# Two weight splits of tick 21 are placed later, and six small products of expert 0 sooner, in a delta-rule and mixture-of-experts kernel

## The chip, the cores and the metric

The kernel runs on one core of a Trainium2 chip. The metric is the device time of one execution in microseconds (us); lower is better. The time before is 500.74 us, the median of 3 runs that lie between 495.13 and 504.34 us.

## The reference

The program computes a linear attention with the delta rule (4 sequences, 8 heads, 768 tokens, head size 48), then a mixture of 8 experts in which each of the 3072 tokens goes to one expert.

```python
k_n = k / (norm(k) + 1e-6)
for t in range(S):                                   # state: D x D for each sequence and head
    y[:, :, t] = q_t @ state
    v_old = state^T k_t
    state = state + beta_t * k_t (v_t - v_old)^T
x = y as (B*S, H*D) = (3072, 384)
e = argmax(x @ w_gate);  g = softmax(x @ w_gate)[e]
out = g * (relu(x @ w1[e]) @ w2[e])                  # w1: 384 x 1024, w2: 1024 x 384, 8 of each
```

## The kernel before

**The scan.** The 768 tokens are cut into 6 blocks of 128, a block of one sequence being a unit (24 units), and each unit into four parts of 32 tokens. A loop of 27 ticks (`for t in range(NN + LAG)`) runs skewed: in tick t, part q of unit t - q is worked on, so that four units are in flight. A tick on TensorE is: the products `ks` of `residual` (L438 with the state, L450 with the units' own updates); VectorE's subtraction of `ks` from the values `v_all` (L457); then `apply`, 64 small products of the solved triangle with `v_all` (L465), which ScalarE copies into the updates `u` (L469); then `finish` of unit t - 3, the output and state products (L488, L499, L508), ScalarE's copies `yt` (L512), and eight products that turn the output into token rows, `xp` (L532). Products `pq` for the next units (L279) are copied by ScalarE into `pm` (L289), which GpSimd masks (L290).

**The work beside it.** Every tick calls `beside(t, i)` for i = 0 to 6. Each call runs some steps of the routing of finished tokens (`emit_slots`: about a dozen VectorE operations that end in a slot number, `sli`, L590 to L615, and then one indirect DMA on GpSimd for each block of rows, which places the rows in the table `xg`, L540), then as many steps of `W` as the table `WSL` says, then steps of expert 0's early work as the table `ES` says. The order is written out by hand: each engine, and SyncE's queue of DMA issues, takes its instructions in program order.

**The weights.** `W` is the generator `pieces()`. A piece of a weight matrix is loaded as fp32 (L739), and `split` makes of it a rounded high part on ScalarE (L724) and the remainder on VectorE (L725), since each product is done as three products of parts. Three raw pieces are kept, so piece k + 3 is loaded behind piece k's split. Expert 0 has pieces 0 to 2 of `w1` (1024 columns) and 3 to 6 of `w2` (768 columns).

**Expert 0's beginning.** Its first 256 rows are worked on before the scan has ended. Their load from `xg` into `xr` (L761) is issued on SyncE behind the routing of unit 17 and waits until the rows placed so far have landed. `early()` transposes them in tick 23 (L816), does the hidden layer (L791, L794, L795) and the output layer (L802), which is made in two halves for the second 128 rows. `rest()` brings in the later rows: 128 by transposes (L854), and then a group of 64 by three products with the identity (L860) and three for each of the last two units, whose rows are taken from SBUF by a selection matrix `one` (L864). The string `EO` orders these steps: x, h and y are steps of `early`, t and o of `rest`; 13 of them stand in `ES`, the others run in the loop that drains the last routing, at the counts in `EF`.

**The experts.** Behind the scan, experts 0 to 7 run one after the other (`ffn`): the hidden layer in eight column groups into three PSUM tiles `hp`, each read by ScalarE and VectorE (`relu`, L794 and L795), and then the output layer (L802, L1146).

## Time and profile before

| what | value |
|---|---|
| median of 3 runs | 500.74 us (495.13 to 504.34) |
| the profiled execution's own time | 502.3 us |
| its span, first to last instruction | 500.5 us |
| mean granted TensorE clock | 0.959 |
| busy: PE, PEld, DVE, ACT, POOL | 92%, 85%, 65%, 53%, 33% |

The page cuts the span into 40 slices; TensorE is at nine tenths or more in nearly all slices of the second half (the experts), and at six to nine tenths in the first (the scan). PE is TensorE's products, PEld its weight loads, DVE is VectorE, ACT ScalarE, POOL GpSimd, SP SyncE, whose queue issues the direct DMAs. Between the span and the execution's own time lie 1.8 us.

### The profile page before, as it was taken

To read this page: it belongs to the slowest core of one execution; us is meant where nothing else is said; L and a number is where in the kernel's file an instruction comes from. 1 tells how busy PE (TensorE), PEld (TensorE's weight loads), DVE (VectorE), ACT (ScalarE), POOL (GpSimd) and SP (SyncE) were. 2 spreads that over 40 slices of the span, in tenths; PEclk is the share of its full clock that TensorE was granted. 3 is DMA by queue.
4 is the path that set the end of the run, shared out by engine and by line. 5 is a ranking of instruction groups with operands and counts; after the bars stand their busy time and mean duration, and the time that the engine had idled before them with its cause. 6 is when DMAs were issued, how large, how long until landed. Compare 5 with 4: busy or idle time off the path is not lost. (4 is left out here: it accounts for less than half of the span.)

```text
span 500.5 us, 17244 instructions
## 1 busy us (share of the span) xinstructions
PE 461.2 (92%) x7212; PEld 425.3 (85%) x7212; DVE 325.3 (65%) x728; ACT 265.6 (53%) x580; POOL 166.5 (33%) x342
## 2 busy tenths in 40 slices
PE   6969797989999799978899999999999999999995
PEld 4958686878887787867798999999999999999995
DVE  5999797698899989555644567465363638255330
ACT  4546694666666565767433356464454546354330
POOL 7002323767877878630211210111102020200202
PEclk9787897999999999999999799999999999999998
DMA  8798569467283433634302548464545637453101
GB/s 246 184 305 201 132 137 265 155 139 192 81 176 119 116 114 99 212 101 152 117 35 65 145 151 248 134 201 123 178 132 153 213 121 218 132 171 112 37 1 45
DMA packets 57147, 73.33 MB, mean 147 GB/s; under 512 B 25929, under 2 KB 44831, under 8 KB 57056
## 3 DMA queue, kind: packets, MB, share of 16 engines
q1 hardware_dynamic: 53600, 62.44, 44.5%
q0 software_dynamic: 3456, 9.57, 5.3%
q8 instruction: 71, 1.16, 0.9%
q14 instruction: 20, 0.16, 0.1%
HBM read 54.15 MB, written 18.62 MB: 145 GB/s over the span
## 5 line engine op out<-in xcount | busy, mean ns | idle before, releaser
L805 POOL DMA_INDIRECT out_dram<-yo,idx x32 | 30.7, 961 | 200.2 <-ACT yo L1140 101.0
L802 PE MATMUL y<-w2h,hx 128*128 128x384 f32 x352 | 93.6, 340 | 0.1
L725 DVE TENSOR_TENSOR w2l<-w2r,w2h 128x768 fp32r<-128x768 f32 x32 | 31.3, 980 | 73.8 <-ACT w2h L724 73.6
L802 PEld LDWEIGHTS y<-w2h,hx 128*128 128x128 f32 x352 | 64.0, 188 | 0.4 <-issue 0.4
L802 PE MATMUL y<-w2l,hx 128*128 128x384 f32 x176 | 59.2, 337 | 0.0
L791 PE MATMUL h<-xl,w1h 128*128 128x416 f32 (+2 forms) x168 | 57.3, 341 | 0.2 <-DVE xl L725 0.2
L791 PE MATMUL h<-xh,w1h 128*128 128x416 f32 (+2 forms) x168 | 57.3, 341 | 0.0
L791 PE MATMUL h<-xh,w1l 128*128 128x416 f32 (+2 forms) x168 | 57.2, 341 | 0.0
L469 ACT COPY u<-ks 32x384 f32<-32x384 f32 x96 | 45.1, 470 | 20.0 <-PE ks L465 18.5
L794 ACT ACTIVATE hx<-h 128x448 fp32r<-128x448 f32 (+1 forms) x64 | 32.9, 517 | 35.6 <-PE h L791 32.2
L1140 ACT ACTIVATE yo<-y,gt 128x384 f32<-128x384 f32 x22 | 12.8, 582 | 68.8 <-PE y L802 57.6
L795 DVE SCALAR_TENSOR_TENSOR hx<-h,hx 128x448 fp32r<-128x448 f32 (+1 forms) x64 | 37.1, 587 | 15.4 <-ACT hx L794 15.1
L290 POOL TENSOR_SCALAR_AFFINE_SELECT pm<-pm 128x1024 f32<-128x1024 f32 x24 | 27.5, 1148 | 56.6 <-ACT pm L289 56.3
L438 PE MATMUL ks<-st,kt 128*32 128x96 f32 x768 | 45.4, 256 | 0.6 <-issue 0.4
L279 PE MATMUL pg<-kt 64*128 64x128 f32 x384 | 34.8, 310 | 9.3 <-ACT gg L261 5.4
L279 PEld LDWEIGHTS pg<-kt 64*128 64x128 f32 x384 | 29.3, 208 | 12.3 <-ACT gg L261 6.3
L438 PEld LDWEIGHTS ks<-st,kt 128*32 128x32 f32 x768 | 33.7, 113 | 4.7 <-issue 1.5
L540 POOL DMA_INDIRECT xg<-row,sli x24 | 28.7, 1197 | 25.2 <-ACT yt L512 8.0
L261 ACT COPY gg<-pg 128x512 f32<-128x512 f32 x48 | 25.7, 587 | 21.4 <-PE pg L279 21.4
L465 PE MATMUL ks<-v_all,wt 32*32 32x48 f32 x1536 | 26.5, 204 | 10.4 <-DVE v_all L457 6.3
L725 DVE TENSOR_TENSOR w1l<-w1r,w1h 128x1024 fp32r<-128x1024 f32 x24 | 29.4, 1224 | 10.2 <-ACT w1h L724 10.1
L465 PEld LDWEIGHTS ks<-v_all,wt 32*32 32x32 f32 x1536 | 21.8, 105 | 15.0 <-DVE v_all L457 7.5
(196 smaller groups left out, 1057.8 us busy)
## 6 DMA issues: line engine op xcount, KB each, us to landing
w1r<-in_w_dram SPq DMA_DIRECT2D x24, 512.0 KB
w2r<-in_w_dram SPq DMA_DIRECT2D x32, 384.0 KB
xg<-zrow SPq DMA_DIRECT2D x7, 788.0 KB
kt<-in_kt_dram SPq DMA_DIRECT2D x17, 256.0 KB
xr<-xg SPq DMA_DIRECT2D x7, 591.0 KB
ku<-in_kn_dram SPq DMA_DIRECT2D x20, 192.0 KB
qt<-in_qt_dram SPq DMA_DIRECT2D x36, 96.0 KB
v_all<-in_v_dram SPq DMA_DIRECT2D x15, 192.0 KB
```

The costliest lines, as they stand in the source:

```text
L279: nc.tensor.matmul(pg[a][:, p], lhsT=kt[r, p], rhs=xt[r, p], start=True, stop=True, tile_position=(64 * a, 0), skip_group_check=True)
L290: nc.gpsimd.affine_select(out=pm, in_=pm, compare_op=ALU.is_gt, fill=0.0, base=0, pattern=[[0, H], [1, C]], channel_multiplier=-1)
L438: nc.tensor.matmul(ks[32 * q:32 * q + 32, 2 * p:2 * p + 2, :], lhsT=kt_t[n % KTL][:, p, 32 * q:32 * q + 32], rhs=st_view(n % B, p), start= ...
L465: nc.tensor.matmul(ks[r, h, :], lhsT=tiles[n // B]["wt"][r, n % B * H + h, :], rhs=vn[r, h, :], start=True, stop=True, tile_position=(32 * ...
L469: nc.scalar.copy(out=uview(n)[r], in_=ks[r])
L540: put = nc.gpsimd.indirect_dma_start(out=xg, out_offset=bass.IndirectOffsetOnAxis(ap=at, axis=0), in_=x, in_offset=None, bounds_check=OFF ...
L725: nc.vector.tensor_tensor(out=lo, in0=src, in1=hi.bitcast(F32), op=ALU.subtract)
L791: nc.tensor.matmul(ps, lhsT=w[:, d, fs], rhs=x_[:, d], start=(n == 0), stop=(n == len(terms) - 1))
L794: nc.scalar.activation(out=hh, in_=ps, func=AF.Relu)
L795: nc.vector.scalar_tensor_tensor(out=hl, in0=ps, scalar=0.0, in1=hh.bitcast(F32), op0=ALU.max, op1=ALU.subtract)
L802: nc.tensor.matmul(ps, lhsT=h(f)[h_], rhs=w2[w][:, f, :], start=(n == 0), stop=(n == len(terms) - 1))
L805: nc.gpsimd.indirect_dma_start(out=out, out_offset=bass.IndirectOffsetOnAxis(ap=idx, axis=0), in_=yo, in_offset=None, bounds_check=N - 1, ...
```

## The change

A piece's split becomes two steps of `W`: ScalarE's copy, then VectorE's subtraction with the next load. `WSL` gives both steps of most pieces the place they had together. Two places differ. Piece 1's split goes from (21, 3) to (21, 5), behind more of the routing's steps. Piece 2's copy stays at (21, 6), and its subtraction and load go to (22, 1), behind tick 22's `residual`. In `rest()`, the step with the small products is cut in two: `p` makes the products with the identity and those of the first of the two units, `o` those of the second unit and the split; `p` stands between the two halves of the last output layer of `early`. The experts' `run(W, 2)` takes both steps of a piece at the place where `run(W)` took one.

```diff
-    WSL = ((20, 3), (21, 3), (21, 6), (22, 3), (22, 6), (23, 3), (23, 6))
+    WSL = ((20, 3), (20, 3), (21, 5), (21, 5), (21, 6), (22, 1), (22, 3), (22, 3), (22, 6), (22, 6), (23, 3), (23, 3),
+           (23, 6), (23, 6))
-    EF = (4, 8, 9, 10, 12, 13, 14, 15)
-    EO = 'xxxhhhhhhhhytyyo'
+    EF = (4, 7, 8, 9, 10, 12, 13, 14, 15)
+    EO = 'xxxhhhhhhhhytypyo'
...
-            split(hi[:, j:j + st], lo[:, j:j + st], raws[k])
+            nc.scalar.copy(out=hi[:, j:j + st], in_=raws[k])
+            yield
+            nc.vector.tensor_tensor(out=lo[:, j:j + st], in0=raws[k], in1=hi[:, j:j + st].bitcast(F32), op=ALU.subtract)
             if k + AH < len(todo):
                 load(k + AH)
             yield
...
-        for i, (row, one) in enumerate(last):
+        for i in range(DEF):
+            if i == DEF - 1:
+                yield
+            row, one = last[i]
             for d in range(KD):
                 nc.tensor.matmul(pt[:, d], lhsT=row[:, d * 128:(d + 1) * 128], rhs=one, start=False,
-                                 stop=(i == len(last) - 1), skip_group_check=True)
+                                 stop=(i == DEF - 1), skip_group_check=True)
...
     def ahead_step():
-        if order and not (order[0] == "o" and len(last) < DEF):
-            run(other if order.pop(0) in "to" else ahead)
+        if order and len(last) >= {"p": 1, "o": DEF}.get(order[0], 0):
+            run(other if order.pop(0) in "tpo" else ahead)
...
-                run(W)
+                run(W, 2)
```

VectorE, ticks 21 and 22, before: `w1l` is the remainder of a piece of expert 0's first matrix (`w1r0_1` is piece 1, `w1r0_2` piece 2), `pos`, `ovr` and `sli` are the routing of units 16 and 17, and `ks22` is what tick 22 subtracts.

```order
L725 TENSOR_TENSOR w1l0_4189<-w1r0_1_4044,w1h0_4188 128x1024
L590 TENSOR_TENSOR pos4_0_4346<-base_77,pp4_0_4341 128x16
L592 TENSOR_TENSOR base_77<-base_77,pp4_0_4341 128x8
L598 TENSOR_TENSOR base_77<-base_77,jump_80 128x8
L600 TENSOR_TENSOR ovr4_0_4347<-pos4_0_4346,lim_78 128x16
L602 TENSOR_TENSOR ovr4_0_4347<-ovr4_0_4347,beyond_79 128x16
L603 TENSOR_TENSOR pos4_0_4346<-ovr4_0_4347,pos4_0_4346 128x16
L605 TENSOR_TENSOR pos4_0_4346<-pos4_0_4346,oh_all_84 128x16
L607 TENSOR_REDUCE sl_all_83<-pos4_0_4346 128x2
L615 CAST sli4_0_4380<-sl_all_83 128x2
L725 TENSOR_TENSOR w1l0_4189<-w1r0_2_4046,w1h0_4188 128x1024
L457 TENSOR_TENSOR v_all_109<-v_all_109,ks22_4386 128x384
```

The same place on VectorE in the changed kernel, from the last routing operation but one on.

```order
L608 TENSOR_REDUCE sl_all_83<-pos4_0_4342 128x2
L751 TENSOR_TENSOR w1l0_4189<-w1r0_1_4044,w1h0_4188 128x1024
L616 CAST sli4_0_4380<-sl_all_83 128x2
L458 TENSOR_TENSOR v_all_109<-v_all_109,ks22_4383 128x384
L535 TENSOR_REDUCE rl4_2_4429<-xp4_2_4430 128x8
L422 TENSOR_TENSOR v_all_109<-v_all_109,nt_all_120 128x384
L751 TENSOR_TENSOR w1l0_4189<-w1r0_2_4046,w1h0_4188 128x1024
L751 TENSOR_TENSOR w2l0_4505<-w2r0_0_4192,w2h0_4504 128x768
```

Piece 1's subtraction has moved from ahead of the routing operations to behind all of them but `sli`, and piece 2's from ahead of tick 22's subtraction to behind it and two more operations. On ScalarE the copy of piece 1 goes from ahead of tick 21's two `yt` copies to behind them, ahead of the `pm` copies; piece 2's copy stays.

SyncE's queue at the same ticks, before: `w2r0_0`, `w2r0_2`, `w2r0_4` and `w2r0_6` are pieces 3, 4, 5 and 6, `xr0` the first rows of expert 0.

```order
L739 DMA w2r0_0_4192<-in_w2_dram 128x2x384
L195 DMA qt5_115<-in_qt_dram 48x512 x2
L739 DMA w2r0_2_4339<-in_w2_dram 128x2x384
L739 DMA w2r0_4_4384<-in_w2_dram 128x2x384
L761 DMA xr0_4446<-xg_60 128x2x394
L739 DMA w2r0_6_4508<-in_w2_dram 128x2x384
```

SyncE's queue in the changed kernel.

```order
L740 DMA w2r0_0_4192<-in_w2_dram 128x2x384
L196 DMA qt5_115<-in_qt_dram 48x512 x2
L740 DMA w2r0_2_4365<-in_w2_dram 128x2x384
L764 DMA xr0_4443<-xg_60 128x2x394
L740 DMA w2r0_4_4446<-in_w2_dram 128x2x384
L740 DMA w2r0_6_4508<-in_w2_dram 128x2x384
```

Piece 5's load now stands behind the load of the rows, which waits for placed rows.

TensorE at the end of expert 0's early work, before: `y0_1` is the output of the second 128 rows (here the end of its second half), `xt4` the small products, `h0` the hidden layer of expert 0's other rows.

```order
L802 MATMUL y0_1_5186<-w2h0_4504,he7_5028 128x384
L802 MATMUL y0_1_5186<-w2l0_4505,he7_5028 128x384
L802 MATMUL y0_1_5186<-w2h0_4504,he7_5028 128x384
L860 MATMUL xt4_5232<-ident_67,xr0_4446 128x64 x3
L864 MATMUL xt4_5232<-one2_5142,row5_2_5055 128x64 x3
L864 MATMUL xt4_5232<-one3_5228,row5_3_5168 128x64 x3
L791 MATMUL h0_5265<-xb0_5149,w1h0_4188 128x192
```

TensorE in the changed kernel, where the second half of `y0_1` begins.

```order
L588 MATMUL pp5_3_5199<-oh_all_84,ones_74 128x8
L863 MATMUL xt4_5205<-ident_67,xr0_4443 128x64 x3
L870 MATMUL xt4_5205<-one2_5142,row5_2_5055 128x64 x3
L805 MATMUL y0_1_5186<-w2h0_4504,he4_4929 128x384
L805 MATMUL y0_1_5186<-w2l0_4505,he4_4929 128x384
```

And where that half ends.

```order
L805 MATMUL y0_1_5186<-w2h0_4504,he7_5028 128x384
L805 MATMUL y0_1_5186<-w2l0_4505,he7_5028 128x384
L805 MATMUL y0_1_5186<-w2h0_4504,he7_5028 128x384
L870 MATMUL xt4_5205<-one3_5235,row5_3_5168 128x64 x3
L794 MATMUL h0_5265<-xb0_5149,w1h0_4188 128x192
```

Two thirds of the small products have moved ahead of the second half; the last third and the hidden layer stay behind it.

## Rows read from the trace of the kernel before

**Rows 1.** The page, busy time and share of the span by engine.

```profile
PE 461.2 (92%) x7212; PEld 425.3 (85%) x7212; DVE 325.3 (65%) x728; ACT 265.6 (53%) x580; POOL 166.5 (33%) x342
```

**Rows 2.** Windows: ticks 20, 21, 22, each from its L465; busy us, clock, DMA.

```profile
205.17:213.13 7.96, 7.45 (x217) 6.36 (x216) 2.44 (x4) 5.56 (x12) 5.95 (x14) 1.00 0.81 277
213.13:222.95 9.82, 7.22 (x222) 6.15 (x221) 6.48 (x21) 7.07 (x15) 2.47 (x2) 1.00 0.29 97
222.95:232.41 9.46, 8.21 (x217) 7.04 (x217) 3.20 (x6) 6.26 (x14) 2.83 (x4) 0.82 0.56 173
```

**Rows 3.** Timeline of PE, ticks 21 to 23: start, length, operation, wait.

```profile
217.72 0.86 PE L438 MATMUL ks<-st,kt 128*32 128x96 f32 x24
...
219.37 1.14 PE L532 MATMUL xp<-esel,yt 128*128 128x104 f32 x8
222.95 0.88 PE L465 MATMUL ks<-v_all,wt 32*32 32x48 f32 x64 [2.44 <-DVE v_all L457]
...
228.74 0.86 PE L438 MATMUL ks<-st,kt 128*32 128x96 f32 x24
...
232.41 0.88 PE L465 MATMUL ks<-v_all,wt 32*32 32x48 f32 x64 [0.88 <-DVE v_all L457]
...
233.82 0.44 PE L816 MATMUL xt<-ident,xr 128*128 128x128 f32 x2
```

**Rows 4.** Timeline of DVE, ticks 21 and 22.

```profile
217.66 1.23 DVE L725 TENSOR_TENSOR w1l<-w1r,w1h 128x1024 fp32r<-128x1024 f32 x1 [2.28 <-ACT w1h L724]
218.80 0.16 DVE L590 TENSOR_TENSOR pos<-base,pp 128x16 f32<-128x16 f32 x1
...
219.48 0.99 DVE L602 TENSOR_TENSOR ovr<-ovr,beyond 128x16 f32<-128x16 f32 x1
...
221.13 0.17 DVE L615 CAST sli<-sl_all 128x2 int32<-128x2 f32 x1
221.21 1.23 DVE L725 TENSOR_TENSOR w1l<-w1r,w1h 128x1024 fp32r<-128x1024 f32 x1
222.35 0.55 DVE L457 TENSOR_TENSOR v_all<-v_all,ks 128x384 f32<-128x384 f32 x1
```

**Rows 5.** Timeline of ACT, ticks 21 and 23.

```profile
216.58 1.04 ACT L724 CAST w1h<-w1r 128x1024 fp32r<-128x1024 f32 x1
217.65 0.65 ACT L512 COPY yt<-yp 128x256 f32<-128x256 f32 x2
218.19 1.09 ACT L289 COPY pm<-pq 128x512 f32<-128x512 f32 x2
...
235.47 0.83 ACT L724 CAST w2h<-w2r 128x768 fp32r<-128x768 f32 x1
```

**Rows 6.** Timeline of POOL, ticks 21 and 22.

```profile
219.35 1.09 POOL L290 TENSOR_SCALAR_AFFINE_SELECT pm<-pm 128x1024 f32<-128x1024 f32 x1 [6.29 <-ACT pm L289]
221.57 1.72 POOL L540 DMA_INDIRECT xg<-row,sli  x1 [1.13 <-DVE sli L615]
...
223.89 0.97 POOL L540 DMA_INDIRECT xg<-row,sli  x1 [0.16 <-issue]
```

**Rows 7.** Timeline of SP, its queue, at the load of expert 0's rows.

```profile
228.41 0.37 SPq L761 DMA_DIRECT2D xr<-xg  x1
```

**Rows 8.** Windows: the stretch behind that load; columns as in rows 2.

```profile
229.50:232.00 2.50, 2.03 (x70) 1.72 (x61) 1.32 (x2) 1.58 (x4) 1.09 (x1) 1.00 0.94 311
```

**Rows 9.** Timeline of PE behind the last small products.

```profile
276.45 1.55 PE L864 MATMUL xt<-one,row 128*128 128x64 f32 x12
278.41 0.92 PE L791 MATMUL h<-xb,w1h 128*128 128x192 f32 x2 [0.41 <-ACT xb L724]
```

**Rows 10.** Windows: expert 0's hidden layer of the later rows, in two stretches.

```profile
278.41:285.50 7.09, 7.05 (x32) 6.88 (x33) 5.61 (x25) 2.40 (x5) 1.27 (x7) 0.52 0.55 154
285.50:290.00 4.50, 4.50 (x42) 4.50 (x41) 3.68 (x13) 2.87 (x8) 0.00 (x0) 1.00 0.73 223
```

**Rows 11.** Timeline of DVE, first read of a hidden tile in that layer.

```profile
282.62 0.36 DVE L795 SCALAR_TENSOR_TENSOR hx<-h,hx 128x192 fp32r<-128x192 f32 x1
```

## The prediction

> **What bounds the kernel now.** I read the page's busy shares first: TensorE is busy 92% of the span [rows 1], and no other engine comes near it, so the kernel ends when TensorE has got through its list, and only what TensorE waits for, or what slows its clock, can be won. I then cut the scan into ticks with the windows view, to see whether the ticks that the change touches are longer than their neighbour. They are: tick 20 takes 7.96 us, tick 21 9.82 and tick 22 9.46, with less TensorE work done per us [rows 2]. The timeline of TensorE names why. Between its last product of tick 21 (L532, from 219.37, 1.14 long) and L465 of tick 22 it stands for 2.44 us, and the trace puts that down to VectorE's subtraction L457 [rows 3]. Then the granted clock falls: it averages 0.82 over the next tick, after 1.00 in the two before [rows 2].
>
> VectorE's timeline shows what L457 stood behind. Piece 1's remainder ran at 217.66, having waited for ScalarE's copy; the routing's small operations came behind it from 218.80 to 221.13; then piece 2's remainder from 221.21; and L457 only at 222.35 [rows 4], though what it subtracts was complete before L532 began at 219.37. None of the work ahead of it is needed by TensorE in tick 22. The second place is expert 0's later rows: behind the small products (twelve of the eighteen instructions take 1.55 us) TensorE waits 0.41 for a copy [rows 9], and then the clock stands at 0.52 for 7.09 us before it is back at 1.00 [rows 10].
>
> **Part one: the wait of tick 22.** In the new order the routing operations start as soon as their products are there, about 2 us before 218.80, and end before piece 1's copy does. ScalarE does the two `yt` copies first (0.65) and then piece 1's copy (1.04) [rows 5]; if `yt` starts where the copy started, at 216.6, or a tenth later when its products are done, the copy ends between 218.3 and 218.5. Piece 1's remainder takes 1.14 to the next operation's start (217.66 to 218.80) [rows 4], so `sli` starts near 219.6 and L457, next behind it, near 219.7; it takes 0.55 and is done at 220.3. TensorE's L532 ends at 220.5. So the wait goes whole: **-2.4 us**. What hides piece 1's remainder now is TensorE's own list from L438 at 217.72 to L532; without that cover it would cost up to its 1.23. Piece 2's remainder, 1.23 us, goes behind L457 and two more operations, into a stretch where VectorE is busy for 3.20 of 9.46 us [rows 2]; nobody needs it before the hidden layer, which comes behind the transposes of tick 23. It costs nothing. ScalarE's `pm` copies come 0.3 later, and GpSimd's mask with them: that is work for a later tick.
>
> **The clock of tick 22.** From L465 to the next L438 tick 21 took 4.59 us (213.13 to 217.72) and tick 22 5.79 (222.95 to 228.74) [rows 2, 3]: 1.2 more, a lower bound since tick 21 has small routing products there that tick 22 lacks. The upper bound is the clock's own: 0.82 over 9.46 us is 3.4 us at half rate, half of it, 1.7, lost [rows 2]. The fall came behind the only wait over 2 us here, and the wait of 0.88 at 232.41 [rows 3] has full-rate work behind it. I take **-1.5 us**.
>
> **What is late next.** Everything behind tick 22 then comes 3.9 us sooner, if its data do. The wait of 0.88 at tick 23's L465 [rows 3] stays, since piece 4's split keeps its place. The new candidate is the load of expert 0's rows, which TensorE transposes at 233.82 [rows 3], so at 229.9 in the changed kernel. The load was issued at 228.41 [rows 7], 4.5 us behind the second placing DMA at 223.89 [rows 6], and had landed by 232.0 together with a weight piece of similar size [rows 8]; the two share 2.5 us, so the rows alone landed between 231.0 and 232.0, 2.6 to 3.6 behind the issue. In the new order `sli` is there 1.3 us sooner, but GpSimd masks until 220.8 (219.35 + 1.09 [rows 6], plus the 0.3), so the first placing DMA starts at 220.8 in place of 221.57 and the second at 222.4 to 223.1 in place of 223.89, the first having taken 0.97 to 1.72 [rows 6]. The rows' load is then issued at 226.9 to 227.6 and landed at 229.5 to 231.2: a new wait between nothing and 1.3 us. The early end is nearer, because piece 5's load, which ran while the placed rows were being written, is now queued behind. I take **+0.3 us**.
>
> SyncE's queue is the other thing to look at: piece 5's load used to be issued before the rows' load, and now it waits with it. It would be issued near 227.5 and land third at most 3.6 to 4.5 later, 231.1 to 232; ScalarE wants it at 235.47 [rows 5] less 3.9, at 231.6. That is cover of half a us or a lack of as much, on an engine that is not the bound. Piece 6, behind it, has a whole half tick more.
>
> **Part two: the small products.** Twelve instructions move ahead of the output layer's second half and six stay. TensorE's work is the same, so nothing is won directly, and the 0.41 wait for the copy stays [rows 9]. What can be won is the clock: 7.09 us at 0.52 are 3.4 us lost [rows 10]. The fall follows the longest run of 64-column products in the neighbourhood and a wait; the change cuts that run in three. I think it more likely than not that the clock then holds. But the 3.4 us are not all to be had. The hidden layer fills three PSUM tiles, and VectorE reads the first only at 282.62 to 282.98 [rows 11], 4.6 us behind the layer's start at 278.41, because a list of small operations that count the experts' rows stands ahead. At full rate (42 instructions in 4.50 us [rows 10], so 0.96 for the nine of a tile) three tiles are full after 2.9 us, and TensorE stands for 1.7. That leaves 1.7 of the 3.4. The last block's rows are also placed later, behind the output's DMA on GpSimd, by up to the length of what was moved (1.6 us: twelve instructions, at the rate of [rows 9]), and expert 1's load waits for them; if that shows, it takes more of this. Bounds: 0 and -3.4; I take **-1.0 us**.
>
> The experts' `run(W, 2)` leaves the order of every engine as it was: nothing.
>
> **A rule against the change.** VectorE's L602 ran 0.99 us where its like take 0.16 to 0.17, from 219.48 to 220.47, while GpSimd's mask ran from 219.35 to 220.44 [rows 4, 6]; it ended when the mask did. The Trainium skill says why, in "SBUF — State Buffer", section "Who interferes with whom": VectorE and GpSimd share a pair of SBUF ports as an exclusive lock, taken by an operation with two SBUF inputs or, in a faster mode, by a copy or cast, and the second to come stands until the first ends. This row agrees for two SBUF inputs; no run here shows a cast. By that rule `sli`, a cast, could meet the mask.
>
> As a mechanism of this kernel that is a rival. `sli` starts at 219.6 and the mask at 219.7. If the mask comes first, `sli` stands until 220.8, L457 runs to 221.4, and TensorE waits 0.95 us: the first term is -1.5 and not -2.4. L457 itself reads PSUM, and ran 0.55 in its normal place as here.
>
> **The sum.** -2.4 - 1.5 + 0.3 - 1.0 = -4.6 us. The profiled execution took 502.3 us; it would take 497.7. It lies 1.6 above the median of 500.74, so the median would be **496.1 us**.
>
> **The rivals.** *All of it.* Both falls of the clock go and nothing is given back: -2.4 - 1.7 - 3.4 = -7.5, 493.2 us. For it speaks that the runs before reach down to 495.13, so the falls may not be in every run; against it the three PSUM tiles.
>
> *A part.* `sli` meets the mask, and the clock of expert 0 falls as before: -1.5 - 1.5 + 0.3 = -2.7, 498.0 us. For it speaks L602; and the small products that stay, with the copy's wait behind them, are still 1.2 us of low work.
>
> *The wait only moves.* The rows land at the late end, TensorE waits 1.3 in tick 23, and tick 22 keeps 0.95: -1.5 - 1.2 + 1.3 = -1.4, 499.3 us.
>
> *Slower.* SyncE's queue decides. If the placed rows land no sooner than before, the rows' load is issued at 228.4 and TensorE stands from 229.9 until 231.0 to 232.0, at the worst 2.1 us; a wait of that length brought the clock down in tick 22, 1.5 more; and piece 5 lands third, a us behind the rows, at 233.0, which holds ScalarE's copies behind it for 1.4. Together 5.0 against the 3.9 won: +1.1, 501.8 us. It decides from a rows' issue later than 228. Against it: the placing DMAs can start sooner.
>
> **How the numbers follow.** The forecast has 0.45, all of it 0.18, a part 0.22, the wait only moved 0.09, slower 0.06. The runs before spread by 9 us, and a median of a few such runs moves by 2 or 3 by itself, which is wider than the unknown terms. With the cases from 493.2 to 501.8 the range is 491.5 to 500.8 us. A measurement of this kernel can tell some 2% (10 us) from no change; none of the cases is that far off, so within 2% gets 0.92, faster 0.06, for all of it in a good draw of the clock elsewhere, and slower 0.02.
>
> **What the changed profile would show.** Right: no wait at tick 22's L465, tick 21 near 7.4 us, the granted clock at 1.00 through tick 22, L465 of tick 23 near 228.5; the rows' load issued near 227 and a wait of less than 0.5 at the transposes; the hidden layer at full clock with a new wait on VectorE before its fourth tile. Wrong: `sli` as long as GpSimd's mask; a wait of over 1 us at L816; clock at half behind the small products as before.

## The result, and the profile after

The changed kernel took 502.16 us (median of 22 runs, 498.52 to 505.65) beside 500.4 us of the kernel before on the same chip. The ratio is 1.0057, with a 95% interval of 1.0033 to 1.008: a little slower, where 496.1 was predicted, and outside the predicted range. (The ratio compares fast runs alone, and the profiled execution of the kernel before, 502.3 us, counts among the slow ones; the medians of all runs are 1.8 us apart.) Run again on another chip it came out at 1.0046 [1.0006, 1.0085].

The page says little: TensorE's share is what it was [rows 1].

```profile
PE 459.6 (92%) x7212; PEld 422.8 (84%) x7212; DVE 325.5 (65%) x728; ACT 264.8 (53%) x580; POOL 166.8 (33%) x342
```

The two executions have to be cut where the change begins. Up to tick 21's `xp` product (L532 before, L533 after) both kernels have the same instructions, and yet the eighteen profiles of this study reach that product between 204.8 and 213.7 us, with falls of the clock in different places. What lies in front of it says nothing of the change. So I count from the start of the `xp` product of tick 21, by which I mean the one directly ahead of tick 21's `apply` (212.06 us before, 212.65 changed); the prediction, which cuts at `apply`, has it at the end of tick 20. First the kernel before, by windows: ticks 21 and 22 together, tick 23, the three ticks up to the last `xp` product, and the rest to the end. Columns as in [rows 2], with GB/s last.

```profile
212.06:230.39 18.33, 15.35 (x437) 13.19 (x436) 8.51 (x23) 12.50 (x27) 5.61 (x7) 0.91 0.40 113
230.39:240.07 9.68, 7.88 (x204) 6.33 (x203) 6.76 (x22) 6.45 (x16) 1.49 (x2) 1.00 0.51 173
240.07:270.18 30.11, 28.25 (x399) 25.09 (x393) 14.52 (x61) 12.13 (x31) 5.68 (x6) 1.00 0.22 66
270.18:500.48 230.30, 223.71 (x1304) 220.13 (x1304) 116.20 (x223) 103.31 (x177) 32.54 (x39) 0.98 0.45 138
```

The same four stretches of the changed kernel.

```profile
212.65:229.22 16.57, 14.92 (x437) 12.39 (x436) 8.67 (x23) 11.57 (x26) 5.74 (x7) 1.00 0.41 126
229.22:239.61 10.39, 7.87 (x203) 6.33 (x202) 6.77 (x22) 7.15 (x17) 1.89 (x2) 1.00 0.54 176
239.61:269.75 30.14, 28.26 (x399) 25.09 (x394) 14.51 (x61) 12.12 (x31) 5.67 (x6) 1.00 0.21 66
269.75:501.34 231.59, 222.55 (x1304) 218.85 (x1304) 116.27 (x223) 103.11 (x177) 32.50 (x39) 0.99 0.44 137
```

The change wins 1.76 us in ticks 21 and 22, loses 0.71 in tick 23 and 1.29 behind the scan: +0.27 in all, less than the 1.8 us between the medians and the 2.9 of the ratio. In the last stretch TensorE is busy for 1.16 us less (the clock stands higher), but idle for 9.04 us in place of 6.59. The second profile of the changed kernel has the same first and last stretch, and in tick 23 a fall of the clock to its lower level, 1.2 GHz (0.66 on the tick's average), with which the tick takes 3.1 us more:

```profile
207.44:224.00 16.56, 14.59 (x438) 12.31 (x437) 8.68 (x23) 11.59 (x26) 5.75 (x7) 1.00 0.36 119
224.00:237.51 13.51, 11.56 (x204) 9.41 (x203) 8.20 (x23) 7.51 (x17) 3.43 (x3) 0.66 0.42 146
267.41:498.91 231.50, 222.37 (x1304) 218.68 (x1304) 116.19 (x223) 103.19 (x177) 32.70 (x39) 0.99 0.42 137
```

Where TensorE stood, by its timeline in the changed kernel (answers to [rows 3, 9]): 0.51 us in place of 2.44 in tick 22, then three short stops; 1.59 in place of 0.88 in tick 23; and a new wait of 2.12 us before the fourth hidden tile of expert 0, on VectorE's `hx`.

```profile
221.60 0.70 PE L466 MATMUL ks<-v_all,wt 32*32 32x48 f32 x44 [0.51 <-DVE v_all L458]
222.63 0.46 PE L466 MATMUL ks<-v_all,wt 32*32 32x48 f32 x20 [0.34 <-issue]
...
224.33 0.27 PE L489 MATMUL yp<-qt,st 64*64 64x128 f32 x1 [0.30 <-issue]
225.01 0.61 PE L500 MATMUL sum<-u,ku 128*64 128x48 f32 x15 [0.41 <-ACT u L470]
...
227.57 0.86 PE L439 MATMUL ks<-st,kt 128*32 128x96 f32 x24
...
231.96 0.88 PE L466 MATMUL ks<-v_all,wt 32*32 32x48 f32 x64 [1.59 <-DVE v_all L458]
...
277.87 0.75 PE L794 MATMUL h<-xb,w1h 128*128 128x192 f32 x2 [0.41 <-ACT xb L725]
...
283.52 0.47 PE L794 MATMUL h<-xb,w1h 128*128 128x192 f32 x2 [2.12 <-DVE hx L798]
...
291.02 0.42 PE L805 MATMUL y<-w2h,hx 128*128 128x384 f32 x1
```

VectorE's timeline names what stood ahead (answers to [rows 4, 11]): in tick 22 the cast `sli`, 1.06 us long where it took 0.17 before; in tick 23 piece 4's remainder; in expert 0 the list of small operations that count the experts' rows (`cnt` to `tot`).

```profile
218.89 1.23 DVE L751 TENSOR_TENSOR w1l<-w1r,w1h 128x1024 fp32r<-128x1024 f32 x1 [1.03 <-ACT w1h L749]
220.03 1.06 DVE L616 CAST sli<-sl_all 128x2 int32<-128x2 f32 x1
221.00 0.54 DVE L458 TENSOR_TENSOR v_all<-v_all,ks 128x384 f32<-128x384 f32 x1
...
230.22 1.22 DVE L751 TENSOR_TENSOR w2l<-w2r,w2h 128x768 fp32r<-128x768 f32 x1 [1.41 <-ACT w2h L749]
231.36 0.54 DVE L458 TENSOR_TENSOR v_all<-v_all,ks 128x384 f32<-128x384 f32 x1
...
280.21 0.17 DVE L1199 TENSOR_TENSOR cnt<-base,e 128x8 f32<-128x8 f32 x1 [0.71 <-issue]
280.56 0.34 DVE L1205 TENSOR_TENSOR cmpt<-cnt,thr 128x168 f32<-128x168 f32 x1 [0.18 <-POOL itr L1213]
...
283.11 0.36 DVE L798 SCALAR_TENSOR_TENSOR hx<-h,hx 128x192 fp32r<-128x192 f32 x1
```

GpSimd's timeline has the two causes (the first line answers to [rows 6]): the mask ran beside the cast, and the constants `e` and `thr`, which the counting needs, stood behind an output transfer that the later second half of the output layer had made late. It begins 0.13 us ahead of the hidden layer's first product; in the kernel before, at 276.61, it began 1.80 ahead [rows 9].

```profile
219.90 1.17 POOL L291 TENSOR_SCALAR_AFFINE_SELECT pm<-pm 128x1024 f32<-128x1024 f32 x1 [5.41 <-ACT pm L290]
...
277.74 0.98 POOL L808 DMA_INDIRECT out_dram<-yo,idx  x1 [6.18 <-ACT yo L847]
279.02 0.97 POOL L541 DMA_INDIRECT xg<-row,sli  x1 [0.31 <-DVE kind L1163]
280.00 0.17 POOL L1198 IOTA e<- 128x8 f32 x1
280.09 0.43 POOL L1203 IOTA thr<- 128x168 f32 x1
```

### The profile page after: what moved, and what is told of

The parts are those of the page before. It is cut to its first block, busy times and chain, and to the rows that moved or that the text cites. A ratio compares the mean times of both kernels' runs of the same rounds, so it can differ in the third digit from the quotient of the medians.

```text
span 501.3 us, 17245 instructions
## 1 busy us (share of the span) xinstructions
PE 459.6 (92%) x7212; PEld 422.8 (84%) x7212; DVE 325.5 (65%) x728; ACT 264.8 (53%) x580; POOL 166.8 (33%) x342
## 3 DMA queue, kind: packets, MB, share of 16 engines
q8 instruction: 71, 1.16, 1.0%
## 5 line engine op out<-in xcount | busy, mean ns | idle before, releaser
L280 PE MATMUL pg<-kt 64*128 64x128 f32 x384 | 36.0, 319 | 10.6 <-DMA kt<-in_kt_dram 5.0
L439 PE MATMUL ks<-st,kt 128*32 128x96 f32 x768 | 44.4, 253 | 0.2
L280 PEld LDWEIGHTS pg<-kt 64*128 64x128 f32 x384 | 30.4, 217 | 13.3 <-ACT gg L262 4.1
L439 PEld LDWEIGHTS ks<-st,kt 128*32 128x32 f32 x768 | 32.7, 111 | 4.0 <-issue 0.9
L466 PE MATMUL ks<-v_all,wt 32*32 32x48 f32 x1536 | 26.8, 206 | 8.9 <-DVE v_all L458 4.3
L466 PEld LDWEIGHTS ks<-v_all,wt 32*32 32x32 f32 x1536 | 22.2, 107 | 13.8 <-DVE v_all L458 6.1
```

The source lines that it names most:

```text
L280: nc.tensor.matmul(pg[a][:, p], lhsT=kt[r, p], rhs=xt[r, p], start=True, stop=True, tile_position=(64 * a, 0), skip_group_check=True)
L439: nc.tensor.matmul(ks[32 * q:32 * q + 32, 2 * p:2 * p + 2, :], lhsT=kt_t[n % KTL][:, p, 32 * q:32 * q + 32], rhs=st_view(n % B, p), start= ...
L466: nc.tensor.matmul(ks[r, h, :], lhsT=tiles[n // B]["wt"][r, n % B * H + h, :], rhs=vn[r, h, :], start=True, stop=True, tile_position=(32 * ...
```

## The experiments

They ran on four chips, numbered 1 to 4, with 12 runs of every kernel and 35 of the kernel before on each chip; ratios are to the kernel before on the same chip. "21+22" and "23" are ticks as cut above, "rest" goes from the last `xp` product to the end, "sum" from tick 21's product to the end; "wait" is TensorE's on `hx` in expert 0's later rows. These five come from the one profiled execution, in us. The changed kernel itself ran on chip 2 and on the chip of the first comparison only, so that e3, e9 and e16 are set against its ratio on other chips.

| kernel | chip | ratio [95%] | 21+22 | 23 | rest | sum | wait |
|---|---|---|---|---|---|---|---|
| before | - | 1 | 18.33 | 9.68 | 230.3 | 288.4 | 0 |
| changed | - | 1.0057 [1.0033, 1.008] | 16.57 | 10.39 | 231.6 | 288.7 | 2.12 |
| e5 changed again | 2 | 1.0046 [1.0006, 1.0085] | 16.56 | 13.51 | 231.5 | 291.5 | 2.10 |
| e1 split alone | 1 | 0.9911 [0.9874, 0.9948] | 15.79 | 10.39 | 228.9 | 284.9 | 0 |
| e6 split again | 2 | 0.9933 [0.9896, 0.9969] | 16.56 | 10.39 | 230.5 | 287.5 | 1.09 |
| e15 split a third time | 4 | 0.995 [0.9909, 0.9991] | 15.16 | 10.39 | 230.6 | 286.1 | 1.09 |
| e2 small products alone | 1 | 0.9996 [0.9958, 1.0035] | 18.82 | 10.81 | 229.9 | 289.4 | 2.11 |
| e3 constants early | 1 | 0.996 [0.9917, 1.0003] | 16.77 | 10.38 | 229.4 | 286.4 | 1.22 |
| e4 piece 1 behind `sli` | 1 | 0.9953 [0.9917, 0.9989] | 15.92 | 10.92 | 228.9 | 285.6 | 1.08 |
| e7 e3, counting late | 2 | 1.0044 [1.0011, 1.0077] | 16.49 | 10.40 | 233.8 | 290.8 | 0.82 + 2.38 |
| e8 split, counting late | 2 | 1.0044 [1.0007, 1.008] | 17.86 | 9.67 | 234.7 | 292.4 | 2.73 |
| e9 changed, counting cut up | 3 | 0.9977 [0.9945, 1.0009] | 16.65 | 10.39 | 228.6 | 285.8 | 0.82 |
| e16 the same again | 4 | 0.9942 [0.9909, 0.9976] | 17.03 | 10.39 | 228.6 | 285.9 | 0.82 |
| e10 split, counting cut up | 3 | 0.9974 [0.9936, 1.0011] | 16.53 | 13.51 | 230.2 | 290.2 | 0 |
| e11 changed, piece 4 moved | 3 | 1.0087 [1.0042, 1.0131] | 16.53 | 9.92 | 232.9 | 289.5 | 2.10 |
| e12 e10, piece 4 moved | 3 | 0.9962 [0.9926, 0.9999] | 18.11 | 12.96 | 227.7 | 288.1 | 0 |
| e13 e9, casts on GpSimd | 4 | 0.995 [0.9911, 0.9989] | 17.67 | 10.39 | 229.3 | 287.3 | 0.82 |
| e14 split, casts on GpSimd | 4 | 0.9937 [0.9904, 0.9971] | 17.28 | 10.38 | 229.1 | 286.6 | 0 |

The letters of the theories are given afresh in each expectation.

### Which half costs: e1 and e2

The split alone goes back to the old small products (in `rest()` too; `ahead_step()` keeps its new test, which without a `p` in `EO` is the old one); the small products alone go back to the old places of the pieces. Other lines are left out here.

```diff
 e1
-    EF = (4, 7, 8, 9, 10, 12, 13, 14, 15)
-    EO = 'xxxhhhhhhhhytypyo'
+    EF = (4, 8, 9, 10, 12, 13, 14, 15)
+    EO = 'xxxhhhhhhhhytyyo'
 e2
-    WSL = ((20, 3), (20, 3), (21, 5), (21, 5), (21, 6), (22, 1), (22, 3), (22, 3), (22, 6), (22, 6), (23, 3), (23, 3),
+    WSL = ((20, 3), (20, 3), (21, 3), (21, 3), (21, 6), (21, 6), (22, 3), (22, 3), (22, 6), (22, 6), (23, 3), (23, 3),
```

Expected of e1: 

> The changed kernel with its new places for the weight splits, but expert 0's small products in one step behind the output layer, as before. Theory A (the moved small products cost: they push the output's DMA, the last rows' DMA and the constants behind them on GpSimd, and VectorE's counting waits for those; the splits gain a little): 1 to 2 us faster than the kernel before, ratio 0.996 to 0.998, wait of tick 22's L465 near 0.5 us in place of 2.4, the hidden layer of expert 0 as before. Theory B (the splits cost, by the blocked cast and the later loads; the small products gain by the clock): 1 to 3 us slower, ratio 1.002 to 1.006.

Expected of e2: 

> The kernel before's places for the weight splits, and the small products cut in two as in the changed kernel. Theory A: 2 to 4 us slower than before, ratio 1.004 to 1.008, with a wait of about 2 us of TensorE on VectorE before the fourth hidden tile of expert 0. Theory B: 1 to 3 us faster, ratio 0.994 to 0.998.

Measured: 0.9911 and 0.9996. The split wins about 4 us by itself, more than theory A had it (0.996 to 0.998). The small products win nothing and lose nothing, which lies in neither theory's range; they bring the wait of 2.11 us on `hx`, the same as in the changed kernel (2.12), but in this profile the clock holds at the hidden layer, ahead of the wait and behind it. The two halves don't add up to the 1.0057 of the whole.

### Whether chips differ: e5 and e6

The changed kernel and the split alone, unchanged, on one chip.

Expected of e5: 

> The changed kernel once more, beside the split alone on one chip. If the two halves add up (the split alone measured 0.991, the small products alone 1.000), it comes out at 0.990 to 0.996 of the kernel before, and the first comparison's 1.006 belongs to that chip's runs, not to the change. If the two halves together cost something that neither has alone, it comes out at 1.003 to 1.008 again, and tick 22 shows once more the 2 us in which ScalarE waits for tick 22's key product (9.3 us between marks, where the split alone has 7.3). The wait before the fourth hidden tile on VectorE's hx comes under both, at 1.5 to 2.2 us.

Expected of e6: 

> The split alone once more (the new places of the weight pieces, expert 0's small products as before). Theory A (the small products are what costs): 0.988 to 0.994 again, no wait on hx in expert 0, and at least 1 us from the changed kernel on the same chip. Theory B (the two kernels are one, and chips differ): within 0.3% of the changed kernel here.

Measured: 1.0046 and 0.9933. The result stands, and the small products cost some 1.1% next to the split (0.6% between the medians of all runs), more than alone. Tick 22 was no peculiarity of the changed kernel: the split alone has the same 16.56 us here, and 15.79 in its first profile. How long each of the two ticks is goes with the chip and not with the kernel: in all eight profiles of the chips 1 and 4 tick 21 is 7.9 to 10.6 us long and tick 22 6.9 to 8.6; in the other ten tick 21 is 7.31 and tick 22 9.2 to 11.0. And against the expectation the split alone has a wait on `hx` here, 1.09 us. The sums of the two profiles differ by some 4 us (287.5 and 291.5): 1.0 in the rest, 3.1 from the clock that fell in tick 23, which only the one profile shows.

### The constants, and the order of piece 1: e3 and e4

e3 writes GpSimd's six constants at tick 25, ahead of the late output transfer (`counters()` holds the moved lines, which are left out here). e4 is the split alone with piece 1's remainder behind the cast `sli`; the edits that it shares with e1 are left out too, and the "first kernel" of its expectation is e1.

```diff
 e3
+        if t == NN + 1:
+            counters()
 e4
-    WSL = ((20, 3), (20, 3), (21, 5), (21, 5), (21, 6), (22, 1), (22, 3), (22, 3), (22, 6), (22, 6), (23, 3), (23, 3),
+    WSL = ((20, 3), (20, 3), (21, 5), (21, 6), (21, 6), (22, 1), (22, 3), (22, 3), (22, 6), (22, 6), (23, 3), (23, 3),
```

Expected of e3: 

> The changed kernel, with the six constants that GpSimd writes behind the last rows' DMA (e0, thr, itr, part, wo1, wo2) written in tick 25 instead. Theory A: VectorE's counting no longer waits for GpSimd, expert 0's first hidden tile is read about 0.9 us sooner behind the layer's start (4.6 in place of 5.6 us), TensorE's wait before the fourth tile falls from 2.1 to about 1.1, and the kernel is about 1 us faster than the changed one: ratio to before 1.002 to 1.005. If the constants don't matter: ratio as the changed kernel's, 1.0057.

Expected of e4: 

> The first kernel of this call, but with piece 1's subtraction one slot later, at (21, 6), so that the cast to the slot numbers (sli) comes ahead of it, and ahead of GpSimd's mask. If the cast was held by the mask: it takes 0.17 us in place of 1.06, tick 22's subtraction starts about 1 us sooner, TensorE's wait at tick 22's L465 goes from 0.5 to nothing, and the kernel is 0.5 to 1 us faster than the first. If the hold doesn't matter for the time, because something later in tick 22 holds the tick anyway: the same as the first kernel.

Measured: 0.996 and 0.9953. With the constants early the wait falls from 2.12 to 1.22 us, the 0.9 that VectorE had stood for GpSimd (0.71 and 0.18 in its timeline above; the 0.71 is put down to issue, but `cnt` starts when `e`, which it reads, is written); the rest of the wait is VectorE's own list. The ratio lies below the expected 1.002 to 1.005: in this profile the clock does not fall behind the shorter wait, and the rest is 2.1 us shorter than in the changed kernel, not 0.9. In e4 the cast runs ahead of the mask and takes 0.17 us, and tick 22's `ks` waits for nothing; yet e4 is no better than the split alone (its interval and that of e1 overlap), where the cast took 1.06 and TensorE, held up by stops of its own in tick 21 (0.53 and 0.37 us), did not wait for VectorE there either.

### The counting moved in one block: e7 and e8

All of it, `kind` too, goes between the fourth and the fifth hidden tile of expert 0 (the expectations say behind the fifth), with the constants at tick 25; `counting()` holds the moved lines, which are left out here.

```diff
+            if e == 0 and t == 4:
+                counting()
```

Expected of e7: 

> The changed kernel with GpSimd's constants written at tick 25 and VectorE's counting (kind, cnt, cmpt, nb, cum, tot) moved behind the fifth hidden tile of expert 0. Theory A: the wait before the fourth hidden tile goes altogether (2.1 us in the changed kernel, 1.2 with the constants early alone), and the stretch from the last mark to the end loses 1.5 to 2.3 us against the changed kernel; the ratio is 0.003 to 0.005 below the changed kernel's. Theory B (the wait is a stand-in for another one, the row load or the weights): the wait stays under another name and the time is within 0.2% of the constants early alone.

Expected of e8: 

> The split alone with the same constants at tick 25 and the counting behind the fifth hidden tile. Theory A: nothing waits for the counting in the split alone, so at most 0.5 us is gained: 0.986 to 0.992 of the kernel before. Theory B (the order of the small products doesn't matter once the counting is out of the way): equal to the changed kernel with the counting late, within 0.3%.

Measured: 1.0044 for both; the expectation of a gain was wrong, and of e8's theories it is B that holds. VectorE's timeline of e8 shows that the block only moved: it stands between two reads of hidden tiles, 284.80 and 288.78, and TensorE's timeline has a wait of 2.73 us for it; the clock falls to 0.53 for 6.8 us, from 287.5 on.

```profile
284.80 0.35 DVE L798 SCALAR_TENSOR_TENSOR hx<-h,hx 128x192 fp32r<-128x192 f32 x1
285.06 0.16 DVE L1211 TENSOR_TENSOR kind<-base,lim 128x8 f32<-128x8 f32 x1
...
287.35 1.32 DVE L1220 TENSOR_TENSOR cum<-cum,nb 128x1 f32<-128x1 f32 x7
...
288.78 0.35 DVE L798 SCALAR_TENSOR_TENSOR hx<-h,hx 128x192 fp32r<-128x192 f32 x1
```

```profile
289.18 0.74 PE L794 MATMUL h<-xb,w1h 128*128 128x192 f32 x2 [2.73 <-DVE hx L798]
```

The rest is 4.2 to 4.4 us longer than in e6 and e3, and the ratios are 0.011 and 0.008 higher (e8 against e6 on one chip, e7 against e3 on two). So the time does answer to the block's place: for the split alone a block behind the fourth tile is worse than one ahead of the first, and for the changed kernel it is no better (e5, on the same chip, has 1.0046).

### The counting cut up: e9, e10 and e16

`kind` goes two operations at a time behind expert 0's first hidden tiles, the other twelve between expert 1's tiles (twenty in all; the expectation's 23 is a miscount). The functions `kinds()` and `counting()`, left out here, hold them, and `kd` and `co` are their steps.

```diff
             run(main)
+            if e == 0:
+                run(kd)
+            elif e == 1:
+                run(co)
```

Expected of e9: 

> The changed kernel with VectorE's counting cut up: kind's eight operations two by two behind the first four hidden tiles of expert 0, and cnt, cmpt, nb, cum, tot behind expert 1's tiles. Theory A (VectorE's block of 23 small operations, 5 us long with its wait for GpSimd, is what holds the fourth hidden tile): no wait on hx over 0.3 us in expert 0, the stretch from the last mark to the end 229.0 us or less (231.5 in the changed kernel), and the whole 2 to 3 us below the changed kernel on this chip: 0.997 to 1.001 of the kernel before. Theory B (the wait moves to the weights' remainders or the rows): the stretch stays over 230.5 us and the ratio at 1.003 or more.

Expected of e10: 

> The split alone with the counting cut up in the same way. Theory A: the split alone waited 0 and 1.1 us for hx in its two profiles, so 0.5 to 1.5 us are gained on it: 0.986 to 0.992 of the kernel before. Theory B: no gain over the split alone, 0.991 to 0.995.

Expected of e16: 

> The changed kernel with the counting cut up, once more. If VectorE's block of counting was all that the changed kernel lost in expert 0: 0.994 to 0.999 of the kernel before and within 0.3% of the split alone. If the first look at it was luck with the clock: 1.002 or more, and 228.6 us from the last mark to the end doesn't come again.

Measured: 0.9977, 0.9974 and 0.9942. The rest of the changed kernel falls from 231.5 to 228.6 us, twice. The first hidden tile is read 3.1 us behind the layer's start (5.2 in the changed kernel) and waits for ScalarE, as VectorE's timeline of e16 shows, where the layer starts at 270.49:

```profile
273.60 0.36 DVE L798 SCALAR_TENSOR_TENSOR hx<-h,hx 128x192 fp32r<-128x192 f32 x1 [2.77 <-ACT hx L797]
273.87 0.16 DVE L1164 TENSOR_TENSOR kind<-base,lim 128x8 f32<-128x8 f32 x1
...
274.53 1.22 DVE L751 TENSOR_TENSOR w1l<-w1r,w1h 128x1024 fp32r<-128x1024 f32 x1 [0.30 <-ACT w1h L749]
275.68 0.35 DVE L798 SCALAR_TENSOR_TENSOR hx<-h,hx 128x192 fp32r<-128x192 f32 x1
```

The wait that I expected to be gone is 0.82 us, now behind a weight piece's remainder (1.22 us). With the counting out of the way the changed kernel is level with the split treated alike (0.9977 and 0.9974 on one chip), and with the split alone on one chip (e16 0.9942, e15 0.995). The split alone gains nothing from it, against what I expected: 0.9974 lies within the 0.9911 to 0.995 of its three measurements and their intervals, and e10's profile, of the slowest of its twelve executions, has the long fall of the clock in tick 23.

Expected of e15, the split alone beside e16: 

> The split alone a third time, on one chip with the changed kernel with the counting cut up. It has no wait for the counting to lose, so both come out the same within 0.3%, at 0.990 to 0.997 of the kernel before; if the split alone is the better one by 0.4% or more, the small products cost something besides the counting.

### Tick 23's wait: e11 and e12

```diff
-    ... (22, 3), (22, 3), (22, 6), (22, 6), (23, 3), (23, 3),
+    ... (22, 3), (22, 3), (22, 6), (23, 1), (23, 3), (23, 3),
```

Expected of e11: 

> The changed kernel with the remainder of weight piece 4 moved behind tick 23's subtraction, as the change itself does for piece 2 and tick 22. If that remainder (1.22 us, in front of the subtraction) makes tick 23's wait, the wait before the products of ks in tick 23 falls from 1.59 to 0.4 to 0.6 us and the tick's mark comes 0.7 to 1.1 us sooner, with no clock fall in tick 23; the ratio is 0.998 to 1.003. If something else holds the subtraction (the copies of u, the row reduction), the wait stays over 1 us.

Expected of e12: 

> The split alone with the counting cut up and the remainder of piece 4 behind tick 23's subtraction. If both waits are costs that add up: 1 to 2 us below the split alone with the counting cut up, 0.982 to 0.990 of the kernel before. If the clock's falls decide and these waits only move them, it is within 0.3% of the split alone with the counting cut up.

Measured: 1.0087 and 0.9962, no gain in either. The wait before `ks` is gone, but the remainder now delays the slots' `oh_all`, and TensorE waits for that: VectorE's and TensorE's timelines of e11.

```profile
226.96 0.95 DVE L751 TENSOR_TENSOR w2l<-w2r,w2h 128x768 fp32r<-128x768 f32 x1
227.83 0.17 DVE L581 TENSOR_TENSOR oh_all<-oh,m 128x16 bf16<-128x16 f32 x1
```

```profile
228.05 0.18 PE L585 MATMUL pp<-oh_all,ltri 128*128 128x16 bf16 x1 [1.96 <-DVE oh_all L581]
```

Tick 23 is 0.47 us shorter (9.92 for 10.39): the wait moved. e11 is also the changed kernel on the chip of e9, but for this one subtraction: 1.0087 with the counting in its old place, 0.9977 with it cut up.

### The cast and the mask: e13 and e14

```diff
-        V.tensor_copy(sli, sl_all[:, cols])
+        (nc.gpsimd if w > 1 else V).tensor_copy(sli, sl_all[:, cols])
```

Expected of e13: 

> The changed kernel with the counting cut up, and the slots' cast (sli) of the two double groups given to GpSimd, where it stands behind GpSimd's mask in the queue. Theory A (the cast on VectorE is held by the mask, 1.06 us where 0.17 is usual, and holds tick 22's subtraction behind it): tick 22's subtraction starts 0.8 to 1.0 us sooner behind the slots' last step, the wait of 0.51 us before the products of ks goes, and the rows' transfers start within 0.3 us of where they did; 0.5 to 1.0 us less over ticks 21 and 22. Theory B (the subtraction itself is then held by the mask): it takes 1 us or more in place of 0.54, and the two ticks stay at 16.5 us. In the whole time both are within the noise: 0.995 to 0.999 of the kernel before.

Expected of e14: 

> The split alone (expert 0's small products and the counting as before) with the same two casts on GpSimd. Theory A: ticks 21 and 22 together 0.5 to 1.0 us below the split alone (15.8 and 16.6 us in its two profiles), 0.988 to 0.993 of the kernel before. Theory B: as the split alone.

Measured: 0.995 and 0.9937, level with e16 and e15 on the same chip. The mechanism is as theory A has it. GpSimd's timeline of e13, then VectorE's: the mask runs from 215.20 to 216.37, the cast takes 0.18 behind it, and the subtraction runs beside the mask in its usual 0.55 us.

```profile
215.20 1.17 POOL L291 TENSOR_SCALAR_AFFINE_SELECT pm<-pm 128x1024 f32<-128x1024 f32 x1 [7.92 <-ACT pm L290]
216.32 0.18 POOL L616 CAST sli<-sl_all 128x2 int32<-128x2 f32 x1
```

```profile
214.19 1.23 DVE L751 TENSOR_TENSOR w1l<-w1r,w1h 128x1024 fp32r<-128x1024 f32 x1 [1.49 <-ACT w1h L749]
215.51 0.55 DVE L458 TENSOR_TENSOR v_all<-v_all,ks 128x384 f32<-128x384 f32 x1
```

TensorE has no wait at tick 22's `ks` in either profile, and tick 22 is 7.08 and 6.87 us long. The changed kernel has 9.26, but most of that difference goes with the chip: with the cast still on VectorE, e1, e15 and e16 have 7.25, 7.25 and 7.45. And ticks 21 and 22 together are no shorter, 17.67 and 17.28, since TensorE stood for 1.9 and 1.6 us in tick 21, as it does in e16, where its timeline names no engine for it:

```profile
208.92 0.62 PE L466 MATMUL ks<-v_all,wt 32*32 32x48 f32 x39 [2.29 <-issue]
```

## Why the prediction was wrong

**Tick 22's wait (-2.4): right in kind, 0.5 too large.** Counted from tick 21's product, the subtraction starts 1.9 us sooner (8.35 us behind it, 10.29 before), but the cast met the mask. That was priced as a rival (-1.5, with a wait of 0.95); the wait left is 0.51, so the term is -1.9. The Trainium skill ("SBUF — State Buffer", section "Who interferes with whom") counts a cast among the VectorE operations that can take the ports shared with GpSimd; the trace agrees with 1.06 us under the mask and, in e4, 0.17 ahead of it. e13 shows the other side, 0.55 for a subtraction with one operand in PSUM.

**The clock of tick 22 (-1.5): a step that failed.** The clock holds now, 1.00 after 0.91, but nothing came of it in this kernel: from `apply` (L465, now L466) to the next tick's first key product (L438, now L439) tick 22 took 5.97 us, 221.60 to 227.57, where it took 5.79 at the low clock [rows 3]. The size was not the error: TensorE's timeline of e1 has the same stretch with the clock at 1.00 and one stop of 0.26 us: 4.53 us, 1.26 less than before.

```profile
214.82 0.86 PE L466 MATMUL ks<-v_all,wt 32*32 32x48 f32 x59
...
219.35 0.86 PE L439 MATMUL ks<-st,kt 128*32 128x96 f32 x24
```

The error is that I let the stretch shrink by the clock's gain as if nothing else stood in it. In the changed kernel three stops of 0.3 to 0.4 us stand there, two of which the trace puts down to issue, and on the chips 2 and 3 such stops came in every kernel. TensorE's busy time in ticks 21 and 22 falls by 0.43 us (15.35 to 14.92) and its idle time by 1.33 (2.98 to 1.65). So the two terms together are -1.76 and not -3.9.

**What is late next (+0.3): the right question, the wrong answer.** The rows' load, GpSimd's placing and SyncE's queue gave no wait in the changed kernel's profiles; the load was issued 13.97 us behind tick 21's product, where it was 16.35 before [rows 7], as SyncE's timeline shows. That is sooner than I had worked out, so the rival "slower" was wrong in its mechanism. In e13 and e15, on chip 4, TensorE did wait for the rows at the transposes, 0.17 and 0.41 us, as long as the term had it.

```profile
226.62 0.38 SPq L764 DMA_DIRECT2D xr<-xg  x1
```

What was late was tick 23's subtraction, behind piece 4's remainder, which started when ScalarE's copy of the piece was done. I had written that its wait of 0.88 stays because piece 4's split keeps its place. The place stayed, but TensorE came there 1.76 us sooner and the products behind the subtraction could start only 1.04 sooner (19.31 us behind tick 21's product, 20.35 before): the wait became 1.59. In two of the profiles with that wait (e5 and e10) the clock then fell, and the tick took 13.51 us; in e4 the tick took 10.92, with the clock at 0.84 on its average.

**Part two (-1.0): wrong sign, and the step with the largest miss (2.3 of the 4.9 us between -4.6 and +0.27).** The difference of the rest lies in expert 0's hidden layer of the later rows. From its first product to the first of the output layer it takes 11.95 us before (278.41 [rows 9] to 290.36) and 13.15 in the changed kernel (277.87 to 291.02); the stretches of the rest ahead of it and behind it agree within 0.2 us. TensorE's timeline of e12, where that layer has neither a wait on `hx` nor a fall of the clock, has 9.21:

```profile
275.97 0.75 PE L794 MATMUL h<-xb,w1h 128*128 128x192 f32 x2 [0.41 <-ACT xb L725]
...
285.18 0.42 PE L805 MATMUL y<-w2h,hx 128*128 128x384 f32 x1
```

So the fall of before, priced at 3.4, cost 2.7. I saw that VectorE's list of counting stands ahead of the first read, and put the stop of TensorE at 1.7 us with the clock up; that wait came, 2.12 long, with 0.15 behind it. And behind the wait the clock fell again, for 3.4 us, as a window of the changed kernel shows (clock 0.64 over its 4 us):

```profile
284.00:288.00 4.00, 3.85 (x22) 3.68 (x22) 3.11 (x8) 0.77 (x3) 0.00 (x0) 0.64 0.93 270
```

That is the remaining 1.7. The prediction has no term for it, though it had read off tick 22 that the clock fell behind a wait of over 2 us. Where it counted -1.0, the layer gives -2.7 + 2.3 + 1.7, or +1.2 with the numbers unrounded.

Two things made the wait. The list cannot start without GpSimd's constants, and these stand behind the output transfer that the change makes later. `cnt` starts 2.34 us behind the layer's start, in place of 1.40, as the timeline of the kernel before shows (GpSimd's transfer, VectorE's `cnt`, TensorE's output layer): 0.9 us, which e3 gives back.

```profile
276.61 0.97 POOL L805 DMA_INDIRECT out_dram<-yo,idx  x1 [4.62 <-ACT yo L844]
...
279.81 0.16 DVE L1193 TENSOR_TENSOR cnt<-base,e 128x8 f32<-128x8 f32 x1
...
290.36 0.42 PE L802 MATMUL y<-w2h,hx 128*128 128x384 f32 x1
```

And a fall of the clock at the layer's start covers the list: at half rate the prediction's three tiles take 5.8 us (an estimate, twice its 2.9), longer than the 4.6 that it read to the end of the first tile's read, and nothing waits. In the three profiles of the split alone the wait is 0 in the one (e1) where the clock fell at the layer's start, and 1.09 in the others; e14, with such a fall and no wait, and e4, with 1.08 and none, agree. In both profiles of the changed kernel the clock fell behind the new wait, at 285 and 283 us; in those of e2 and e3 it did not, and what decides that is not shown. The rest became 1.3 longer, and in e9 and e16, where the list is cut up, it is 2.9 shorter than in the changed kernel and 1.7 shorter than before. That e3, e7 and e8 move with the list's place as well makes the list the shown cause of what the changed kernel loses in the rest, and e15 and e16 together show that the small products cost nothing else that 12 runs can tell.

**The rivals.** "A part" had the cast right; none had the counting's delay by GpSimd as a loss. That the change would be within 2% was right.

**What stays open.** The stops of 0.2 to 2.3 us that the trace puts down to issue come mostly in tick 21 on the chips 1 and 4 and in tick 22 on the others; ticks 21 and 22 of the split alone took 15.16, 15.79 and 16.56. What sets them is not shown. Nor is why the split and the small products together cost more than the sum of e1 and e2: the wait on `hx` is the same in e2 and in the changed kernel, and one profile each can't give the share of executions in which the clock falls behind it, or in tick 23. If the fall of tick 23 came in half of the changed kernel's executions, as in one of its two profiles, it would add 1.6 us to the +0.27 (an estimate from those two), which comes to the 1.8 between the medians and not to the 2.9 of the ratio.

The best measured kernels are the split alone (0.991, 0.993, 0.995; 0.994 with the casts on GpSimd) and the changed kernel with the counting cut up (0.998, 0.994); against the kernel before that is 2.5 to 4.4 us and 1.1 to 2.9 us, the 1.1 not certain by its interval.

## What to carry to other kernels

A low clock hides other engines' lists: before the loss of a slow stretch is counted as gain, lay the other engines' next operations beside it at full rate, and count what releases them in turn (here GpSimd's constants, behind a transfer that the change itself made late). Count too that the wait which comes to light can bring the clock down again, as it did here. A block of small operations on the engine that empties PSUM was cheap here only in pieces; moved whole, it took its wait along. And when the item ahead of a wait moves, look at the next such wait: it grows by what TensorE gains and the other engine doesn't.

## What was not expected of the hardware

A cast of two columns, 128x2, took 1.06 us on VectorE in place of 0.17 because GpSimd's mask had begun 0.13 us before it; on GpSimd, behind the mask, the same cast took 0.18. And before any instruction that the change touches, the same program comes to tick 21 at times up to 9 us apart (204.8 to 213.7), with the clock's falls in other places: one profile can't price a change of 3 us unless it is cut at the change, and even so cut, the three profiles of the split alone are 2.6 us apart (284.9 to 287.5).
